# Copies of batch 0 moved to VectorE, three ties in the order of the work, and a priority for two instructions of the feed forward

## The chip, the cores and the metric

The kernel runs on one core of a Trainium2 chip. The metric is the device time of one execution in microseconds (us); less is better. A core has TensorE (matrix products, its weight loads are listed apart), VectorE, ScalarE, GpSimd and SyncE, each with an instruction queue that it works through in order, and 16 DMA engines. The times of the kernel before are from three runs; one further execution was profiled.

## The reference

The program is pooled attention followed by a mixing step by Fourier transforms and a feed forward. Shapes: 8 batches, 8 heads, 576 rows, head size 64; 512 channels, 2048 hidden units. The two feed-forward weights come as 64-bit floats, all else as 32-bit floats.

```python
# attention: keys and values are averaged over groups of 8 rows (72 groups)
k_p = k.reshape(B, H, 72, 8, D).mean(axis=3)
v_p = v.reshape(B, H, 72, 8, D).mean(axis=3)
scores = matmul(q, k_p.transpose(0, 1, 3, 2)) / sqrt(D)
x = softmax(scores) @ v_p                    # then heads side by side: (8, 576, 512)
# mixing and feed forward
u = x + real(fft(fft(x, axis=1), axis=2))
un = (u - mean(u)) / sqrt(var(u) + 1e-6)     # over the 512 channels
out = u + maximum(un @ w_ch1, 0) @ w_ch2
```

## The kernel before

Everything is kept with channels on the partitions and rows along the free axis. Each batch b has a *front end*, the generator `fe(b)`: it loads queries and keys for four pairs of heads (g = 3, 2, 0, 1), averages the keys, makes scores (`psS`), a softmax (`t`), transposes of it (`psT`, `psV`, `psR`), the product with the averaged values (`psX`, function `values`), the Fourier transform as products with cosine and sine matrices (`psA`, `psB`, then `psQ`, `psP`), the mean and the variance. Its result is `un`, split into a high part `unh` and a low part `unl`.

The *feed forward* `ffn` runs over blocks of 288 or 384 rows and, in each, over 128 hidden units at a time (a step, f). A step makes `g` with 12 products of 128x128 weights (high with high, high with low, low with high), then `hh` = relu(g) rounded on ScalarE (L779) and `hl` = relu(g) - hh on VectorE (L780), and adds 12 products of `hh` and `hl` with the second weights to four accumulators `acc`. The second half of a step (`gemm2`) comes after the next step's `g`. Batch 0 goes through four blocks: first half and second half of its rows for f 0 to 7, then both for f 8 to 15.

The *weights* come in 34 pieces (`load_w`, `prep_w`), alternately of the first and the second matrix, 512 KB each. A piece in its staging slot (`wst`) is turned into a 32-bit float by two ScalarE activations (L196, L198) and two VectorE instructions (L201 picks the sign, L202 merges), rounded into its high half on ScalarE (L206: `w1h`, `w2h`), and GpSimd subtracts (L207). The low half is stored to memory (L208) and loaded again for each step (L217: `w1low`, `w2low`). Pieces share staging slots, so a load waits until the slot's piece has been merged.

*What sets the order.* The scheduler of the framework walks a simulated time line: on each engine it issues, of the instructions that are ready, the one that was traced first. The order within a queue is fixed when the program is built. `tc.issue_after(x)` ties what is traced within it behind `x` in the queue of `x`'s engine (only the order, without a wait for its end); instructions on other engines are not tied. `behind` holds the instructions that serve as anchors: `behind["R", 0]` is batch 0's last copy of `psR` on ScalarE, `behind["E", 0]` a subtraction on VectorE ahead of `psA`, `behind["X", 0]` the subtraction of the mean from the first half of batch 0's rows (VectorE), `behind["z", 0]` the last of the four `unl` subtractions of that half (VectorE). `HOLD` and `HOLDV` name, for a piece of weights, the anchor behind which its ScalarE activations and its L201 are tied. Batch 1's reductions on VectorE are tied behind `z` already (`apart`). Batch 0's second half (`unfold`) is tied behind `z` as well.

Batch 0's front end is traced first, then the first 11 pieces of weights, then batch 1's front end with the start of batch 2's, then the feed forward, in which each step also advances the front ends of later batches. `keep_busy` puts filler matmuls (`idle`) on TensorE at named places of batch 0's front end.

Of the kernel before, what the change touches and what calls it, by code (L numbers as in the profile page):

```python
# [55 lines left out]
BUSY = {"start": 8, "S3": 3, "S2": 7, "S0": 9, "S1": 4, "T3": 3, "T0": 6, "R": 4, "X": 10, "A": 3, "P": 6, "M": 8}  # L56

HOLD = {2: "R", 3: "R", 4: "R", 5: "R", 6: "B", 7: "B", 8: "B"}
HOLDV = {4: "E", 5: "E", 6: "X", 7: "X", 8: "X"}

EARLY = [4, 6]

# [24 lines left out]
def tile_kernel(ctx: ExitStack, tc: tile.TileContext, qt, kt, vm, vr, w1, w2, cad, cbd, mkd, out):  # L87
# [93 lines left out]
    def prep_w(n):  # L181
        if n >= len(pieces):
            return
        i, f, c, w, _ = pieces[n]
        cl = slice(c * P, (c + w) * P)
        if wide:
            st = staged.pop(n)
            hi = st[:, :, :, 1]
            halves = st.bitcast(U16)
            d0 = wk.tile([P, DM], I32, tag="w", bufs=7, name="wd")[:, 0:w * P]  # L190
            di = d0.rearrange("p (c m) -> p c m", m=P)
            dh = d0.bitcast(U16).rearrange("p (c m h) -> p c m h", m=P, h=2)
            d0 = d0.bitcast(F32)

            with tc.issue_after(behind[HOLD[n], 0].ins) if n in HOLD else ExitStack():
                nc.scalar.activation(hi.bitcast(F32), hi.bitcast(F32), AF.Copy, scale=REBIAS)  # L196

                nc.scalar.activation(dh[:, :, :, 0], st.bitcast(U8)[:, :, :, 3], AF.Copy, scale=1.0 / 32.0, bias=-15.5 / 32.0)  # L198

            with tc.issue_after(behind[HOLDV[n], 0].ins) if n in HOLDV else ExitStack():  # L200
                nc.vector.tensor_scalar(out=dh[:, :, :, 1], in0=halves[:, :, :, 3], scalar1=0x8000, scalar2=None, op0=ALU.bitwise_and)  # L201
            nc.vector.scalar_tensor_tensor(out=di, in0=hi, scalar=3, in1=di, op0=ALU.logical_shift_left, op1=ALU.bitwise_or)  # L202
        else:
            d0 = staged.pop(n)
        wh = high(i, f)[:, cl]
        nc.scalar.copy(out=wh, in_=d0)  # L206
        nc.gpsimd.tensor_tensor(out=d0, in0=d0, in1=raw(wh), op=ALU.subtract)  # L207
        nc.sync.dma_start(wls[i][:, f, cl], d0)  # L208
        for m in after.get(n, ()):
            load_w(m)  # L210
# [39 lines left out]
    def fe(b):  # L250
# [85 lines left out]
        def scores(gi, i):  # L336
# [10 lines left out]
            for c0, n in ((0, 3), (3, 2)):  # L347
                ps = bank(b, f"psS{b}_{g}_{c0}")
                for c in range(n):
                    r0 = SROW[c0 + c]  # L350
                    mm = nc.tensor.matmul(ps[:, c * W2J:(c + 1) * W2J], lhsT=q[:, r0:r0 + P], rhs=kpb[g % 2], start=True, stop=True)  # L351
                if b == 0 and c0:
                    keep_busy(BUSY[f"S{g}"], mm)
                pv = ps[:, 0:n * W2J].rearrange("p (c h j) -> p c h j", h=2, j=J)
                with apart():
                    nc.vector.tensor_reduce(out=mx[:, c0:c0 + n], in_=pv, op=ALU.max, axis=AX.X, negate=(b, g) in SM)  # L356
                if (b, g) in SM:
                    nm = mx[:, c0:c0 + n]
                    nc.vector.tensor_scalar(out=nm, in0=nm, scalar1=1.0 / 64.0, scalar2=None, op0=ALU.mult)
                    for c in range(n):  # L360
                        for h in range(2):
                            x = (slice(None), c0 + c, slice(h, h + 1))
                            nc.scalar.activation(t[:, c0 + c, h], pv[:, c, h], AF.Exp, scale=1.0 / 64.0, bias=mx[x], accum_out=sm[x])
                else:
                    nc.vector.tensor_tensor(out=t[:, c0:c0 + n], in0=pv, in1=mx[:, c0:c0 + n].unsqueeze(3).broadcast_to([P, n, 2, J]), op=ALU.subtract)  # L365
# [63 lines left out]
        def values(g):  # L429
            ah, al = st["a"][g]  # L430
            wh, wl = st["w", g]
            for cl in halves:
                ps = bank(b, f"psX{b}_{g}")[:, 0:HS]
                if b in NAT:
# [5 lines left out]
                if b == 0 and g == 1 and cl.start:  # L440
                    keep_busy(BUSY["X"], last)
                if g == 3:
                    nc.scalar.copy(out=Xb[:, O0, cl], in_=ps)
                    nc.scalar.copy(out=Xb[0:1, E1, cl], in_=ps[0:1])
                elif g == 2:
                    nc.scalar.copy(out=Xb[:, O1, cl], in_=ps)
                    nc.scalar.copy(out=Xb[0:1, O0, cl], in_=ps[0:1])
                    nc.scalar.copy(out=Xb[0:1, O1, cl], in_=Xb[0:1, E1, cl])
                else:
                    e = 2 * g  # L450
                    nc.vector.tensor_tensor(out=Xb[:, e, cl], in0=ps, in1=Xb[:, e + 1, cl], op=ALU.add)
                    nc.vector.tensor_tensor(out=Xb[:, e + 1, cl], in0=ps, in1=Xb[:, e + 1, cl], op=ALU.subtract)
# [114 lines left out]
        for i, m in enumerate(shares):  # L567
            if b:
                channels(i, m, 0)
            ps, _ = channels(i, m, 1)  # L570
            if i < 2:
                parts((AB[i],), ps, 258)
            else:
# [172 lines left out]
    def ffn(ro, nb, to, f0, f1):  # L746
# [15 lines left out]
        for f in range(f0, f1):  # L762
# [13 lines left out]
                    n += 1  # L776
            hh = wk.tile([P, 384], F32R, tag="hh", bufs=2, name="hh")[:, 0:nb]
            hl = wk.tile([P, 384], F32R, tag="hl", bufs=2, name="hl")[:, 0:nb]
            nc.scalar.activation(hh, ps, AF.Relu)  # L779
            nc.vector.scalar_tensor_tensor(out=hl, in0=ps, scalar=0.0, in1=raw(hh), op0=ALU.max, op1=ALU.subtract)  # L780
            yield
            if prev:
                gemm2(f - 1, *prev)
# [214 lines left out]
```

## Time and profile before

| | us |
|---|---|
| median of three runs | 1086.92 (1086.22 to 1087.01) |
| profiled execution | 1087.56 |
| its span, first to last instruction | 1085.6 |
| TensorE busy | 1051.1 (97%) |
| VectorE busy | 615.3 (57%) |
| ScalarE busy | 414.0 (38%) |
| GpSimd busy | 256.0 (24%) |

In the profile PE is TensorE, PEld its weight loads, DVE VectorE, ACT ScalarE, POOL GpSimd and SP SyncE. Busy time is the time that instructions cover; the idle time before an instruction is put down to what released it last. The granted clock is the share of TensorE's full clock. Matmuls overlap, so the mean time of one is longer than the distance from one to the next. L446 is line 446 of the kernel before; tiles go by their names in the program.

### The profile page before, as it was taken

The numbers are of one execution on the slowest core, as the hardware profiler recorded it, in microseconds if no ns is written. First come the engines' busy times: TensorE is split into PE (matmuls) and PEld (weight loads), VectorE is DVE, ScalarE is ACT, GpSimd is POOL, SyncE is SP. The second block draws the span as 40 slices with busy tenths as digits, with TensorE's granted clock in tenths as the row PEclk, the third lists the DMA queues.
The fourth block names the chain that finished last, engine by engine and source line by source line (L and its number), as shares of the span: only waits on it lengthen the run. The fifth ranks groups of instructions, "written<-read, shape, count | busy, mean of one in ns | idle before, by whom it ended". The sixth has DMA issues, their size and how long they took to land.

```text
span 1085.6 us, 17737 instructions
## 1 busy us (share of the span) xinstructions
PE 1051.1 (97%) x6626; PEld 1016.3 (94%) x6626; DVE 615.3 (57%) x1233; ACT 414.0 (38%) x1083; POOL 256.0 (24%) x264
## 2 busy tenths in 40 slices
PE   8878898999999999999999999999999999999998
PEld 7667688999999999999999999999999999999997
DVE  6698877855376455656376455756467434522122
ACT  5868754443244331533243431443324422311110
POOL 6626365211240032311141032300231101300000
PEclk9889999999999999999999999999999999999999
DMA  8859876655345444444444444445435333346563
GB/s 310 257 186 319 282 259 211 201 177 159 113 120 165 131 153 138 128 141 157 136 124 148 133 150 137 139 131 160 140 106 156 97 106 120 116 129 191 163 190 100
DMA packets 91909, 175.80 MB, mean 162 GB/s; under 512 B 10160, under 2 KB 17328, under 8 KB 91568
## 3 DMA queue, kind: packets, MB, share of 16 engines
q1 hardware_dynamic: 91248, 171.71, 51.0%
q0 software_dynamic: 288, 2.66, 0.6%
q8 instruction: 52, 0.85, 0.3%
q10 hardware_dynamic: 288, 0.30, 0.1%
q14 instruction: 33, 0.27, 0.1%
HBM read 156.81 MB, written 17.83 MB: 161 GB/s over the span
## 4 chain that ended last, share of the span: by engine, by line
PE 86%; DVE 5%; ACT 3%; DMA 3%; POOL 1%; issue 1%; SPq 0%; DVEq 0%; POOLq 0%; ACTq 0%
PE g L775 35%; PE acc L759 35%; PE psX L439 3%; PE psS L351 3%; PE psA L558 2%; PE psP L601 2%; PE psB L584 1%; PE psQ L601 1%; PE psT L392 1%; DMA w2l<-wd 1%; POOL wd L207 1%; DMA w1low<-w1l 1%; ACT wd L198 1%; DMA k<-in_kt 1%; PE psR L415 1%
## 5 line engine op out<-in xcount | busy, mean ns | idle before, releaser
L779 ACT ACTIVATE hh<-g 128x384 fp32r<-128x384 f32 (+1 forms) x208 | 96.6, 464 | 338.1 <-PE g L775 318.4
L780 DVE SCALAR_TENSOR_TENSOR hl<-g,hh 128x384 fp32r<-128x384 f32 (+1 forms) x208 | 108.8, 523 | 189.1 <-ACT hh L779 184.2
L759 PE MATMUL acc<-hh,w2h 128*128 128x384 f32 (+1 forms) x832 | 187.2, 327 | 0.9 <-ACT hh L779 0.7
L759 PE MATMUL acc<-hh,w2low 128*128 128x384 f32 (+1 forms) x832 | 187.3, 327 | 0.0
L775 PE MATMUL g<-unh,w1low 128*128 128x384 f32 (+1 forms) x832 | 181.1, 331 | 4.6 <-DMA w1low<-w1l 4.6
L759 PE MATMUL acc<-hl,w2h 128*128 128x384 f32 (+1 forms) x832 | 182.2, 327 | 0.9 <-DVE hl L780 0.8
L775 PE MATMUL g<-unl,w1h 128*128 128x384 f32 (+1 forms) x832 | 178.2, 328 | 3.0 <-DVE unl L646 3.0
L775 PE MATMUL g<-unh,w1h 128*128 128x384 f32 (+1 forms) x832 | 172.4, 326 | 3.1 <-DVE hl L780 2.3
L775 PEld LDWEIGHTS g<-unh,w1low 128*128 128x128 f32 x832 | 140.1, 190 | 7.8 <-DMA w1low<-w1l 5.9
L759 PEld LDWEIGHTS acc<-hh,w2h 128*128 128x128 f32 x832 | 142.9, 188 | 2.7 <-ACT hh L779 1.8
L775 PEld LDWEIGHTS g<-unh,w1h 128*128 128x128 f32 x832 | 139.7, 189 | 4.6 <-DVE hl L780 2.8
L775 PEld LDWEIGHTS g<-unl,w1h 128*128 128x128 f32 x832 | 139.9, 189 | 4.3 <-DVE unl L646 3.7
L759 PEld LDWEIGHTS acc<-hh,w2low 128*128 128x128 f32 x832 | 143.1, 188 | 0.4 <-issue 0.4
L759 PEld LDWEIGHTS acc<-hl,w2h 128*128 128x128 f32 x832 | 141.6, 189 | 2.0 <-DVE hl L780 1.8
L371 POOL TENSOR_TENSOR t<-t,sm 128x720 f32<-128x720 f32 x32 | 47.4, 1482 | 267.4 <-DVE sm L370 247.2
L286 POOL TENSOR_TENSOR k<-k 128x288 f32<-128x288 f32 (+1 forms) x56 | 37.5, 670 | 84.7 <-DMA k<-in_kt 66.5
L638 POOL TENSOR_TENSOR U<-X,U 128x576 f32<-128x576 f32 (+1 forms) x14 | 19.2, 1375 | 120.3 <-DVE X L620 119.6
L356 DVE TENSOR_REDUCE mx<-psS 128x6 f32<-128x432 f32 x64 | 33.0, 526 | 22.9 <-PE psS L351 22.5
L351 PE MATMUL psS<-kpb,q 128*128 128x144 f32 x280 | 43.3, 291 | 1.6 <-DVE t L365 1.6
L351 PEld LDWEIGHTS psS<-kpb,q 128*128 128x128 f32 x280 | 40.1, 194 | 2.2 <-DVE t L365 1.8
L368 DVE TENSOR_REDUCE sm<-t 128x10 f32<-128x720 f32 x31 | 27.9, 901 | 13.1 <-ACT t L367 12.7
L798 POOL TENSOR_TENSOR U<-U,X 128x288 f32<-128x288 f32 x2 | 1.6, 798 | 140.9 <-DVE X L793 140.9
(218 smaller groups left out, 1466.4 us busy)
## 6 DMA issues: line engine op xcount, KB each, us to landing
w1low<-w1l SPq DMA_DIRECT2D x208, 256.0 KB, 2.7
w2low<-w2l SPq DMA_DIRECT2D x208, 256.0 KB, 2.9
wst<-in_w SPq DMA_DIRECT2D x30, 512.0 KB, 5.1
k<-in_kt SPq DMA_DIRECT2D x28, 288.0 KB, 3.1
q<-in_qt SPq DMA_DIRECT2D x28, 288.0 KB, 3.4
v<-in_vm SPq DMA_DIRECT2D x28, 256.0 KB, 2.9
out<-U SPq DMA_DIRECT2D x18, 384.0 KB, 3.5
w1l<-wd SPq DMA_DIRECT2D x16, 256.0 KB, 4.6
```

What stands on the lines that cost most here:

```text
L286: behind["k" if n == 1 and src.shape[1] == J else "v", b] = nc.gpsimd.tensor_tensor(out=out if n == 1 else src[:, :, 0:n], in0=src[:, :, 0 ...
L351: mm = nc.tensor.matmul(ps[:, c * W2J:(c + 1) * W2J], lhsT=q[:, r0:r0 + P], rhs=kpb[g % 2], start=True, stop=True)
L356: nc.vector.tensor_reduce(out=mx[:, c0:c0 + n], in_=pv, op=ALU.max, axis=AX.X, negate=(b, g) in SM)
L368: nc.vector.tensor_reduce(out=sm, in_=t, op=ALU.add, axis=AX.X)
L371: ins = nc.gpsimd.tensor_tensor(out=t, in0=t, in1=sm.unsqueeze(3).broadcast_to([P, 5, 2, J]), op=ALU.mult)
L439: last = nc.tensor.matmul(ps, lhsT=w, rhs=a, start=(i == 0), stop=(i == len(mm) - 1))
L558: last = nc.tensor.matmul(ps, lhsT=w, rhs=a, start=(n == 0), stop=(n == len(mm) - 1))
L601: last = nc.tensor.matmul(ps, lhsT=w, rhs=a, start=(i == 0), stop=(i == 6))
L759: mm = nc.tensor.matmul(acc[e], lhsT=w[:, e], rhs=h, start=(f == f0 and x == 0), stop=(f == f1 - 1 and x == 2))
L775: nc.tensor.matmul(ps, lhsT=w[:, c], rhs=x[:, ti, cl], start=(n == 0), stop=(n == 11))
L779: nc.scalar.activation(hh, ps, AF.Relu)
L780: nc.vector.scalar_tensor_tensor(out=hl, in0=ps, scalar=0.0, in1=raw(hh), op0=ALU.max, op1=ALU.subtract)
```

## The change

- In `values`, the copies of `psX` into `X` for head pairs 3 and 2 run on VectorE for batch 0 (ten copies: for each half of the rows, two for g = 3 and three for g = 2). For the other batches they stay on ScalarE.
- In `prep_w`, the rounding of pieces 0 and 1 into their high halves (L206) is tied behind `behind["R", 0]` on ScalarE.
- `HOLDV` ties the sign conversion (L201) of pieces 6, 7 and 8 behind `z` instead of `X`.
- In `scores`, batch 1's first score matmul for g = 3 is tied behind batch 0's last `psA` matmul on TensorE, which `channels` now hands out as `behind["psA", b]`.
- In `ffn`, the instructions of `hh` and `hl` are traced at high priority: of the ready instructions of ScalarE and VectorE the scheduler takes them first, as if they stood at the start of the program.

No instruction is added or taken away.

```diff
--- before.py
+++ after.py
@@ -56,7 +56,7 @@
 BUSY = {"start": 8, "S3": 3, "S2": 7, "S0": 9, "S1": 4, "T3": 3, "T0": 6, "R": 4, "X": 10, "A": 3, "P": 6, "M": 8}
 
 HOLD = {2: "R", 3: "R", 4: "R", 5: "R", 6: "B", 7: "B", 8: "B"}
-HOLDV = {4: "E", 5: "E", 6: "X", 7: "X", 8: "X"}
+HOLDV = {4: "E", 5: "E", 6: "z", 7: "z", 8: "z"}
 
 EARLY = [4, 6]
 
@@ -203,7 +203,8 @@
         else:
             d0 = staged.pop(n)
         wh = high(i, f)[:, cl]
-        nc.scalar.copy(out=wh, in_=d0)
+        with tc.issue_after(behind["R", 0].ins) if n < 2 else ExitStack():
+            nc.scalar.copy(out=wh, in_=d0)
         nc.gpsimd.tensor_tensor(out=d0, in0=d0, in1=raw(wh), op=ALU.subtract)
         nc.sync.dma_start(wls[i][:, f, cl], d0)
         for m in after.get(n, ()):
@@ -348,7 +349,9 @@
                 ps = bank(b, f"psS{b}_{g}_{c0}")
                 for c in range(n):
                     r0 = SROW[c0 + c]
-                    mm = nc.tensor.matmul(ps[:, c * W2J:(c + 1) * W2J], lhsT=q[:, r0:r0 + P], rhs=kpb[g % 2], start=True, stop=True)
+
+                    with tc.issue_after(behind["psA", 0].ins) if b == 1 and g == 3 and c + c0 == 0 else ExitStack():
+                        mm = nc.tensor.matmul(ps[:, c * W2J:(c + 1) * W2J], lhsT=q[:, r0:r0 + P], rhs=kpb[g % 2], start=True, stop=True)
                 if b == 0 and c0:
                     keep_busy(BUSY[f"S{g}"], mm)
                 pv = ps[:, 0:n * W2J].rearrange("p (c h j) -> p c h j", h=2, j=J)
@@ -429,6 +432,7 @@
         def values(g):
             ah, al = st["a"][g]
             wh, wl = st["w", g]
+            copy = nc.scalar.copy if b else nc.vector.tensor_copy
             for cl in halves:
                 ps = bank(b, f"psX{b}_{g}")[:, 0:HS]
                 if b in NAT:
@@ -440,12 +444,12 @@
                 if b == 0 and g == 1 and cl.start:
                     keep_busy(BUSY["X"], last)
                 if g == 3:
-                    nc.scalar.copy(out=Xb[:, O0, cl], in_=ps)
-                    nc.scalar.copy(out=Xb[0:1, E1, cl], in_=ps[0:1])
+                    copy(out=Xb[:, O0, cl], in_=ps)
+                    copy(out=Xb[0:1, E1, cl], in_=ps[0:1])
                 elif g == 2:
-                    nc.scalar.copy(out=Xb[:, O1, cl], in_=ps)
-                    nc.scalar.copy(out=Xb[0:1, O0, cl], in_=ps[0:1])
-                    nc.scalar.copy(out=Xb[0:1, O1, cl], in_=Xb[0:1, E1, cl])
+                    copy(out=Xb[:, O1, cl], in_=ps)
+                    copy(out=Xb[0:1, O0, cl], in_=ps[0:1])
+                    copy(out=Xb[0:1, O1, cl], in_=Xb[0:1, E1, cl])
                 else:
                     e = 2 * g
                     nc.vector.tensor_tensor(out=Xb[:, e, cl], in0=ps, in1=Xb[:, e + 1, cl], op=ALU.add)
@@ -567,7 +571,7 @@
         for i, m in enumerate(shares):
             if b:
                 channels(i, m, 0)
-            ps, _ = channels(i, m, 1)
+            ps, behind["psA", b] = channels(i, m, 1)
             if i < 2:
                 parts((AB[i],), ps, 258)
             else:
@@ -776,8 +780,9 @@
                     n += 1
             hh = wk.tile([P, 384], F32R, tag="hh", bufs=2, name="hh")[:, 0:nb]
             hl = wk.tile([P, 384], F32R, tag="hl", bufs=2, name="hl")[:, 0:nb]
-            nc.scalar.activation(hh, ps, AF.Relu)
-            nc.vector.scalar_tensor_tensor(out=hl, in0=ps, scalar=0.0, in1=raw(hh), op0=ALU.max, op1=ALU.subtract)
+            with tc.high_priority():
+                nc.scalar.activation(hh, ps, AF.Relu)
+                nc.vector.scalar_tensor_tensor(out=hl, in0=ps, scalar=0.0, in1=raw(hh), op0=ALU.max, op1=ALU.subtract)
             yield
             if prev:
                 gemm2(f - 1, *prev)
```

## Rows read from the trace of the kernel before

**Rows 1.** The page: busy time, share of the span and instructions of each engine.
```profile
PE 1051.1 (97%) x6626; PEld 1016.3 (94%) x6626; DVE 615.3 (57%) x1233; ACT 414.0 (38%) x1083; POOL 256.0 (24%) x264
```

**Rows 2.** Stretches: window, length, busy us (instructions) of each engine, clock, DMA share, GB/s.
```profile
29.00:36.70 7.70, 4.69 (x27) 2.95 (x25) 1.31 (x3) 7.65 (x25) 4.64 (x9) 1.00 0.81 268
36.70:46.10 9.40, 9.36 (x37) 7.08 (x38) 8.82 (x15) 6.58 (x16) 6.87 (x8) 0.64 0.82 250
...
57.00:64.00 7.00, 4.61 (x35) 4.02 (x33) 6.90 (x17) 2.40 (x5) 0.00 (x0) 1.00 0.07 27
...
69.50:79.00 9.50, 7.79 (x34) 7.32 (x35) 9.50 (x19) 7.92 (x21) 1.97 (x2) 0.68 0.84 264
79.00:95.00 16.00, 13.26 (x89) 11.68 (x87) 15.85 (x30) 14.95 (x48) 11.28 (x7) 0.99 0.94 311
95.00:130.00 35.00, 28.29 (x183) 23.68 (x184) 27.60 (x56) 27.47 (x69) 17.44 (x15) 1.00 0.94 331
...
200.00:985.00 785.00, 785.00 (x4829) 773.56 (x4829) 438.82 (x888) 272.12 (x715) 147.31 (x137) 1.00 0.45 137
```

**Rows 3.** Who waited for whom: us in total, times, longest us.
```profile
ACT hh L779 <- PE g L775: 318.4, 144, 5.6
...
PE g L775 <- DMA w1low<-w1l: 4.6, 5, 1.5
PE psV L405 <- ACT rt L379: 3.9, 2, 2.6
PE g L775 <- DVE unl L646: 3.0, 2, 1.5
PE g L775 <- DVE hl L780: 2.3, 2, 1.9
...
PE acc L759 <- DVE hl L780: 0.8, 2, 0.5
...
PE acc L759 <- ACT hh L779: 0.7, 2, 0.5
```

**Rows 4.** Chain that ended last, 29 to 46 us: start, length, what.
```profile
29.15 0.40 ACT X L446
...
29.57 0.62 ACT w1h L206
...
33.98 0.33 ACT X L448
...
36.74 3.82 PE psX L439 x8
...
45.12 1.27 PE psS L351 x10
```

**Rows 5.** VectorE in order of time, 36 to 78 us: start, length, what, idle before.
```profile
36.00 1.01 DVE L451 TENSOR_TENSOR X<-psX,X 128x288 f32<-128x288 f32 x2 [6.29 <-PE psX L439]
...
63.35 1.13 DVE L201 TENSOR_SCALAR wd<-wst 128x512 uint16<-128x512 uint16 x3
...
67.38 1.76 DVE L202 SCALAR_TENSOR_TENSOR wd<-wst,wd 128x512 int32<-128x512 int32 x1
...
69.80 1.90 DVE L638 TENSOR_TENSOR U<-X,U 128x288 f32<-128x288 f32 x2
...
73.69 0.81 DVE L639 TENSOR_TENSOR U<-X,U 128x288 f32<-128x288 f32 x2
...
76.70 1.33 DVE L661 TENSOR_TENSOR X<-U,psM 128x1152 f32<-128x1152 f32 x1
```

**Rows 6.** Groups by line and shape: busy us, mean ns, idle before.
```profile
L451 DVE TENSOR_TENSOR X<-psX,X 128x288 f32<-128x288 f32 x28 | 12.5, 455 | 18.6 <-PE psX L439 18.2
...
L446 ACT COPY X<-psX 128x288 f32<-128x288 f32 x14 | 5.4, 386 | 9.4 <-PE psX L439 9.3
```

**Rows 7.** The same chain, 91 to 105 us.
```profile
91.52 4.91 DMA w2l<-wd
...
100.34 4.28 DMA w1low<-w1l
```

## What I expected before the result

> **What bounds the kernel now.** I read the page first: TensorE is busy 1051.1 of 1085.6 us, so 34.5 us are left in which it does nothing [rows 1]. Then the table of stretches, to see where they lie [rows 2]: from 200 to 985 us it is busy 785.00 of 785.00 at full clock, and nothing that another engine does faster can shorten that part. The loss lies ahead of 200 us: 7.70 us of time with 4.69 of work at 29 to 36.7, granted clocks of 0.64 and 0.68 in 36.7 to 46.1 and 69.5 to 79, and from 79 to 130 TensorE busy 13.26 of 16 and 28.29 of 35, while VectorE is nearly full (15.85 of 16, 27.60 of 35) and the DMA engines are at 0.94. Third, TensorE's waits by cause [rows 3]: low weight halves 4.6 us, the `rt` copy on ScalarE 3.9, `unl` 3.0, `hl` 2.3 and 0.8, `hh` 0.7. Fourth, the chain of work around batch 0's values and VectorE's list of instructions there [rows 4, 5]: from 29.15 until `psX` begins at 36.74 the chain lies on ScalarE without a gap, and VectorE meanwhile sat idle for 6.29 us. Last, the chain through the feed forward's first steps [rows 7]: it runs through the weight preparation and its round trip to memory, not through TensorE.
>
> The profiled execution took 1087.56 us, 1.96 more than its span; the median of the runs is 0.64 less. I sum against the profiled one and put the same difference on the median.
>
> **Part 1: batch 0's ten copies to VectorE, and two conversions behind `R`.** The chain on ScalarE holds six of the ten copies between 29.15 and 34.31 (first and last in [rows 4]; 0.40 + 3 x 0.29 + 0.32 + 0.33 = 1.92 us) and the two conversions `w1h` and `w2h` of pieces 0 and 1 (the first 0.62, so about 1.2). All leave the chain that ends in `wh`, on which the last eight `psX` matmuls wait: 3.1 us. The other four copies lie before it, in a stretch that waits for GpSimd anyway: nothing. The moved conversions take along their subtraction on GpSimd, the store and the reload of the low half; the first low half is wanted by step 0 near 70 us, over 30 us later, so that costs nothing. VectorE gets ten copies. How long one takes there no row shows; the nearest is the sum out of the same PSUM tile and shape, 455 ns against 386 ns for the copy on ScalarE [rows 6]; a copy has one input less, so between 386 and 455: 3.9 to 4.55 us in all. The cover is the 6.29 us of idle time ahead of the first sum [rows 5]; as that sum comes 3.1 us sooner, 3.2 are left, and 0.7 to 1.3 us of copies run over, less what slips in before 27 us. I take 0.7 of cost. The net is -2.4 us. Bounds: -1.7, and on the other side -5.0, when `rt` is copied at once, TensorE's 3.9 us of `psV` waits shrink, and the last eight `psX` matmuls (3.82 us in a stretch with clock 0.64) run at nearly full clock.
>
> The Trainium skill speaks against this part: VectorE: DVE Perf Modes, the section on the TRN2 errata, has a fixed cost plus one cycle a column for both engines, 120 cycles at 0.96 GHz on VectorE and 172 at 1.2 GHz on ScalarE out of PSUM. My estimate from it for 288 columns is 425 ns against 383; the trace agrees for ScalarE (386) and has no such copy on VectorE. By that figure each copy is dearer by 0.04 us, the ten take 4.25, and the sum would move by less than 0.2 us.
>
> **Part 2: batch 1's first score matmuls behind batch 0's last `psA`.** They stand as 1.27 us between the filler matmuls and `psA` on the chain [rows 4]. Their readers on VectorE are tied behind `z` near 69 us anyway, so nobody misses them. If they fall into TensorE's wait at 57 to 64 us, the 1.27 are won; if they land between `psA` and `psB`, nothing. I take -1.0.
>
> **Part 3: three sign conversions behind `z` instead of `X`.** Before, VectorE did three of them (1.13 us) directly after `X` and then wove their merges (the third 1.76 us) between the four `unl` subtractions [rows 5]. TensorE waited 3.0 us for `unl` in two pieces [rows 3]. The tie takes all six instructions out of that place: up to -3.0. But they are done later by the same engine, which is full from 69.5 to 95 us [rows 2], and every later `hl`, score and conversion queues behind. I take half, -1.5. Bounds: 0 (VectorE alone decides) and -6.0, when TensorE's clock no longer falls either: 0.68 over 9.5 us is 3.04 us lost.
>
> **Part 4: `hh` and `hl` first.** It matters only where TensorE waits for them: 2.3 + 0.8 + 0.7 = 3.8 us, all before 200 us [rows 3]. Later ScalarE stands waiting for `g` before most of them (144 of 208 times, 318.4 us [rows 3]), so being first changes nothing there. What is pushed back on VectorE are batch 1's scores and the weights' merges, which are due soon too; half is kept: -2.0, with bounds -3.8 and 0.
>
> **Part 5: what is given back.** Feed-forward steps that come earlier ask for low halves earlier. These come by ScalarE, VectorE, GpSimd, a store of 4.91 us and a load of 4.28 [rows 7], with the DMA engines at 0.94 from 79 to 130 us. Against it, the DMA engines stood at 0.07 from 57 to 64 us [rows 2], so the stream itself can start earlier with everything else. The 4.6 us of waits for low halves grow by 0 to 4; I take +1.0, near the lower end, because the whole front shifts together.
>
> **The sum**: -2.4 - 1.0 - 1.5 - 2.0 + 1.0 = -5.9 us. 1087.56 - 5.9 = 1081.7 profiled, 1086.92 - 5.9 = 1081.0 for the median.
>
> **The rivals.** (a) Given back in full: VectorE and the DMA engines are full from 79 to 130 us, so TensorE only comes sooner to the same weights; waits for `w1low` grow from 4.6 to about 9. For it: [rows 7] and the DMA share of 0.94. Against: the stretch begins with idle DMA engines. About -1, 1086.0. (b) Slower: behind `z` VectorE has more than the three pieces ready; if it takes the second half's unfold (1.90 + 0.81 us), its subtraction of the mean (1.33) [rows 5] and four `unl` first (like the 455 ns of [rows 6], 1.8), 5.8 us in all, pieces 6 to 8 come 5.8 us later, counted from `z`, than before. Parts 1 and 2 give 3.4 of that back. Piece 6 carries step 3, and its staging slot the load of piece 10; 2.4 us later there, with a DMA stretch at 0.94 behind it that can't catch up, and parts 3 and 4 then hidden behind that wait: +2.4, 1089.3. It decides from the point where that delay is above the gain of the start. (c) The priority changes no order that matters: -3.9, 1083.0. (d) Everything joins: both stretches of low clock go, the start gains 5.0 and `unl` with its clock 4.5, and `hl` 2.5: -12, 1075.
>
> **How the numbers follow.** Forecast, 1078 to 1084.5: 0.46. (a) 0.17, (b) 0.15, (c) 0.10, (d) 0.12. The range reaches from (d) to (b), 1074.5 to 1089.0; the outer halves of both are left out. About 0.2%, 2.2 us, is what a measurement can tell from no change here: faster 0.68 (forecast, c, d), same 0.17, slower 0.15.
>
> **What the changed profile would show.** Part 1 right: the last `psX` of batch 0 ends near 38 us instead of 40.6, the copies stand on VectorE at about 0.4 us, and the 6.29 us of idle time there are gone; wrong if `psX` then waits for VectorE. Part 2: `psA` begins without `psS` before it. Part 3: no wait for `unl` at step 0, and the merges of pieces 6 to 8 behind the fourth `unl`. Part 4: the 3.8 us of waits for `hh` and `hl` below 2. Part 5: the waits for `w1low` beside 4.6 us; above 9, (a) or (b) holds, and (b) if pieces 6 to 8 are merged later than 69 us. From 200 us on TensorE should again show no gap; if it does, the priority has put something in the wrong order and the forecast fails there. The plainest test is when TensorE's last long wait ends: 5 to 6 us earlier than the 200 us of before.

## The result: 1096.9 us, slower, and the profile after

The changed kernel takes 1096.87 us, median of 4 runs (1092.88 to 1098.38), against 1086.72 for the kernel before: a ratio of 1.0086, 95% interval 1.0061 to 1.0110. The forecast was 1081.0 with a range up to 1089.0, so both the sign and the range failed. The profiled execution took 1092.88 us, span 1091.1.

The stretches of the changed kernel, in the windows of [rows 2]: window, length, busy us (instructions) of TensorE, its weight loads, VectorE, ScalarE and GpSimd, granted clock, DMA share, GB/s.

```profile
29.00:36.70 7.70, 7.41 (x45) 5.79 (x43) 4.61 (x14) 6.66 (x17) 5.06 (x8) 1.00 0.95 353
36.70:46.10 9.40, 4.31 (x22) 4.16 (x23) 9.34 (x13) 5.24 (x13) 6.59 (x6) 0.64 0.85 271
57.00:64.00 7.00, 4.96 (x34) 4.25 (x34) 6.40 (x16) 2.27 (x6) 0.00 (x0) 1.00 0.01 2
69.50:79.00 9.50, 8.47 (x44) 8.40 (x44) 9.50 (x18) 7.09 (x16) 5.64 (x4) 0.64 0.90 307
79.00:95.00 16.00, 10.58 (x65) 10.16 (x63) 13.66 (x23) 14.77 (x46) 13.33 (x9) 0.79 1.00 348
95.00:130.00 35.00, 29.61 (x177) 24.80 (x175) 28.00 (x62) 27.48 (x69) 13.79 (x13) 0.92 0.92 321
200.00:985.00 785.00, 780.17 (x4765) 766.45 (x4764) 432.94 (x874) 266.67 (x706) 146.74 (x137) 1.00 0.44 135
```

Three things are to be seen. From 29 to 36.7 us TensorE now works 7.41 of 7.70 us, but directly behind it only 4.31 of 9.40, where it had worked 9.36. From 79 to 95 us it works 10.58 of 16 at a clock of 0.79, where it had 13.26 at 0.99, and the DMA engines are full. And from 200 to 985 us, where before has not one gap, 4.83 us are idle. TensorE's waits of the changed kernel, by cause (us in total, times, longest us):

```profile
PE g L779 <- DMA w1low<-w1l: 7.5, 3, 3.5
PE psA L562 <- ACT f L515: 5.4, 1, 5.4
PE acc L763 <- DVE hl L785: 3.5, 1, 3.5
...
PE psS L354 <- DVE X L665: 2.4, 1, 2.4
PE g L779 <- DVE unl L650: 2.2, 2, 1.3
...
PE acc L763 <- ACT hh L784: 0.6, 1, 0.6
```

Against [rows 3], `psV`'s wait for `rt` fell from 3.9 to 0.2 us, `unl` at step 0 is gone (the 2.2 us of `unl` here are another wait, at 822 to 827 us), and in their place stand 5.4 us for `f`, 3.5 in one piece for `hl`, and 7.5 for `w1low` instead of 4.6.

**Where the time came from.** A program is best followed by the feed forward's own products: 4992 matmuls (`g` and `acc`), of which I note when the nth starts. Up to product 1200 and up to product 4200 the same amount of front-end work lies behind TensorE in every kernel (but for a dummy product or two, and in e12 for 12 front-end products that come behind the first mark instead of ahead), so those two marks can be compared directly. The times are read to 0.1 us, so differences of them are good to 0.1. Before reaches product 1200 at 332.0 us and needs 641.8 us from there to 4200. The changed kernel reaches it at 328.7, 3.3 earlier, and needs 650.6. So in the profile the front gained 3.3 us, and then 8.8 were lost where nothing should have changed: 5.5 in all, and the spans differ by 5.5 (1091.1 - 1085.6). In the median of the runs the loss is 10.2. If the late loss is the same in each execution, which only the profiled one shows, the front did not gain in most of them.

The late loss lies at one place. The chain of work that ended last in the changed kernel, 814 to 832 us (start, length, what):

```profile
815.67 0.14 PE psM L661
...
815.91 1.35 DVE X L665
817.26 0.81 DVE sm L371
818.07 1.86 DVE acc L809 x4
819.94 1.25 DVE X L665
...
822.25 1.39 DVE U L810 x3
...
823.76 1.39 DVE unl L650
...
826.04 1.02 DVE unl L650
...
827.11 4.26 PE g L779 x14
```

These are batch 6's rows: `psM` gives their mean, VectorE subtracts it (L665) and makes `unl` (L650), and the feed forward's `g` reads them. Feed-forward products from number 3457 on need them, and in TensorE's queue batch 6's last `psM` stands exactly behind product 3456. At the same moment a block of the feed forward ends, and VectorE also has its eight accumulator operations (L809 and L810), a softmax and batch 7's scores to do, in between. TensorE stands still. The same work on VectorE in the kernel before (start, length, instruction):

```profile
807.17 1.34 DVE L661 TENSOR_TENSOR X<-U,psM 128x1152 f32<-128x1152 f32 x1
...
809.10 1.29 DVE L661 TENSOR_TENSOR X<-U,psM 128x1152 f32<-128x1152 f32 x1
...
811.13 1.43 DVE L646 TENSOR_TENSOR unl<-X,unh 128x576 fp32r<-128x576 f32 x2 [0.74 <-ACT unh L645]
...
823.10 1.50 DVE L804 TENSOR_TENSOR acc<-acc,rb 128x384 f32<-128x384 f32 x3 [2.92 <-PE acc L759]
```

There the last `psM` stands behind product 3388, 68 products or 11.8 us (68 x 0.174, a 384-column product's pace at full clock) ahead of the need, and the rows are ready 10 us before the accumulator operations begin. Of the changed kernel's 8.8 us, 7.8 lie between 818.0 and 831.2 us: ten `psS` and 24 `g` matmuls start in these 13.2 us, which at their pace at full clock (0.124 and 0.174 us from start to start) would be 5.4. Of the 7.8, 4.6 are idle time in three pieces. Then ten `g`, from 827.5 to 830.4 us, start 0.32 us apart instead of 0.174; the granted clock is 0.67 at 828 to 832 us. The rest is slower starts around the waits, and about 1 us is spread over the other products.

### The profile page after: what moved, and what is told of

Read it like the earlier page. It is cut to its first block, busy times and chain, and to the rows that moved or that the text cites. A ratio compares the mean times of both kernels' runs of the same rounds, so it can differ in the third digit from the quotient of the medians.

```text
span 1091.1 us, 17716 instructions
## 1 busy us (share of the span) xinstructions
PE 1051.3 (96%) x6626; PEld 1019.7 (93%) x6626; DVE 616.7 (57%) x1243; ACT 410.1 (38%) x1073; POOL 256.7 (24%) x264
## 4 chain that ended last, share of the span: by engine, by line
PE 87%; DVE 6%; DMA 4%; issue 1%; ACT 1%; POOL 0%; SPq 0%; DVEq 0%; POOLq 0%; ACTq 0%
PE acc L763 36%; PE g L779 36%; PE psX L443 3%; PE psS L354 3%; PE psA L562 2%; PE psP L605 2%; PE psB L588 1%; PE psQ L605 1%; PE psT L395 1%; DMA wst<-in_w 1%; DMA w1low<-w1l 1%; DVE wd L202 1%; PE psR L418 1%; DVE wd L201 1%; DMA w1l<-wd 1%
## 5 line engine op out<-in xcount | busy, mean ns | idle before, releaser
L763 PE MATMUL acc<-hh,w2h 128*128 128x384 f32 (+1 forms) x832 | 189.8, 330 | 0.6 <-ACT hh L784 0.6
L779 PE MATMUL g<-unh,w1low 128*128 128x384 f32 (+1 forms) x832 | 178.7, 330 | 7.6 <-DMA w1low<-w1l 7.5
L779 PE MATMUL g<-unh,w1h 128*128 128x384 f32 (+1 forms) x832 | 177.8, 329 | 0.7 <-ACT unh L649 0.7
L370 ACT ACTIVATE t<-t 128x720 f32<-128x720 f32 x31 | 24.9, 803 | 36.4 <-DVE t L368 36.3
```

Of the source, the lines that this page charges most:

```text
L370: nc.scalar.activation(t, t, AF.Exp, scale=1.0 / 64.0)
L763: mm = nc.tensor.matmul(acc[e], lhsT=w[:, e], rhs=h, start=(f == f0 and x == 0), stop=(f == f1 - 1 and x == 2))
L779: nc.tensor.matmul(ps, lhsT=w[:, c], rhs=x[:, ti, cl], start=(n == 0), stop=(n == 11))
```

## The experiments

Three theories at first. **O**: the built order of the later batches is the whole loss. **W**: the weights, pushed back by the ties behind `z`, lose it in the front. **P**: the priority of `hh` and `hl` pushes the front ends back. The table is the outcome; "psM 6" is the number of feed-forward products ahead of batch 6's last `psM` in TensorE's queue (the expectations count to the first of the four, 16 fewer: 3372 for 3388, 3440 for 3456). Behind product 1200 the matmuls stand in one and the same order on TensorE in before, e6, e7, e10 and e15, and in another that e2, e5 and e14 share; ahead of it the order differs from kernel to kernel (e15 is e10 again). The two columns of us come from the profiled execution, the medians and ratios from all runs. In the last two groups of runs (e9 to e15) the kernel before itself varied more, medians of 1087.7 and 1087.8, so the ratios are what to compare there.

| kernel | parts | psM 6 | product 1200 at | 1200 to 4200 | median | ratio to before (95%) |
|---|---|---|---|---|---|---|
| before | none | 3388 | 332.0 | 641.8 | 1086.7 | 1 |
| after | 1 2 3 4 | 3456 | 328.7 | 650.6 | 1096.9 | 1.0086 (1.0061-1.0110) |
| e2 | 1 3 4 | 3388 | 331.4 | 641.9 | 1090.1 | 1.0036 (1.0022-1.0050) |
| e3 | 4 | 3456 | 332.1 | 650.6 | 1097.0 | 1.0101 (1.0081-1.0120) |
| e4 | 1 2 4 | 3456 | 331.1 | 650.5 | 1096.0 | 1.0086 (1.0061-1.0111) |
| e5 | 1 2 3 4, a dummy more | 3388 | 332.2 | 642.0 | 1092.9 | 1.0048 (1.0032-1.0064) |
| e6 | 1 3 | 3388 | 335.9 | 641.8 | 1091.0 | 1.0038 (1.0026-1.0051) |
| e7 | 1 | 3388 | 328.3 | 641.8 | 1086.1 | 0.9998 (0.9989-1.0007) |
| e8 | 1 2 3 | 3456 | 332.3 | 649.0 | 1094.9 | 1.0080 (1.0062-1.0097) |
| e9 | 1 2, a dummy more | 3388 | 332.4 | 641.8 | 1089.6 | 1.0009 (0.9987-1.0032) |
| e10 | 1 4, a dummy more | 3388 | 329.9 | 641.8 | 1084.6 | 0.9964 (0.9942-0.9986) |
| e11 | 1 2 4, a dummy more | 3388 | 333.9 | 641.7 | 1088.5 | 1.0006 (0.9983-1.0030) |
| e12 | 1, piece 6 early | 3440 | 341.5 | 647.6 | 1099.6 | 1.0104 (1.0063-1.0145) |
| e13 | 1 4 | 3456 | 328.8 | 650.5 | 1094.1 | 1.0065 (1.0043-1.0088) |
| e14 | 1 2 3 4, a dummy less | 3388 | 336.6 | 642.0 | 1092.6 | 1.0054 (1.0032-1.0075) |
| e15 | e10 again | 3388 | 331.0 | 641.8 | 1084.4 | 0.9971 (0.9953-0.9989) |

**e1, batch 6's front end earlier by hand.** It lets batch 6's front end start two places earlier (a feed-forward step has two). It then overwrites rows that batch 4's last steps still read, so part of those steps is computed from other rows.

```diff
-free = {1: 0, 2: 64, 3: 128, 4: 160, 5: 224, 6: 256, 7: 320}
+free = {1: 0, 2: 64, 3: 128, 4: 160, 5: 224, 6: 254, 7: 320}
```

> The whole change stays; only the place from which batch 6's front end goes on is set 2 positions earlier (254 instead of 256), so TensorE's queue is the same as in the changed kernel until batch 6. There batch 6's last psM comes after 3176 feed-forward products instead of 3440, where its rows are wanted at 3456. Theory O (the later order: the front of the changed kernel is some 4.8 us ahead until 720 us, and all of the loss comes from batch 6's rows being ready too late, at 817 to 831 us): 10 us less than the changed kernel's profiled 1092.9, so about 1082, with no wait of TensorE from 200 to 985 us. Theory W (the weights in front: pieces 6 to 8 done late, low halves late): the time stays at 1090 or more. Theory P (hh and hl at the highest priority push the front ends back in all steps): 1090 or more as well.

Measured: 1108.5 us, where O expected about 1082 and no wait. The edit moved batch 6's last `psM` from behind product 3456 to behind 3190, and its front end was crammed together: TensorE waited 4.5 us for `f`, 2.0 for `R` and 1.1 for `f` again between 730 and 785 us, and the clock was 0.50 from 760 to 770. W and P expected 1090 or more, but not for this reason, so it decides nothing between the theories. It shows that a front end can also stand too early and too close.

**e2, without the tie on the scores (part 2).**

```diff
-with tc.issue_after(behind["psA", 0].ins) if b == 1 and g == 3 and c + c0 == 0 else ExitStack():
-    mm = nc.tensor.matmul(...)
+mm = nc.tensor.matmul(...)
```

> The change without part 2 (batch 1's first scores are not tied behind psA). In the built program batch 6's last psM then comes after 3372 feed-forward products, as before the change, though parts 1, 3 and 4 are all in. Theory O: 1080 to 1084, no wait for unl after 200 us. Theory W: about 1095, as pieces 6 to 8 are as late as in the changed kernel. Theory P: about 1095, as the priority is in.

Measured: 1090.1. Its built order puts batch 6 back behind 3388 products, and 1200 to 4200 takes 641.9 us as in before. The late loss is gone although the priority and the ties behind `z` are still there, where W and P expected it unchanged. But 3.4 us of loss remain in the runs, against O's 1080 to 1084: there is a second loss, and the profile leaves no place for it behind product 1200.

**e3, the priority alone on the kernel before (part 4).**

```diff
-nc.scalar.activation(hh, ps, AF.Relu)
-nc.vector.scalar_tensor_tensor(out=hl, ...)
+with tc.high_priority():
+    nc.scalar.activation(hh, ps, AF.Relu)
+    nc.vector.scalar_tensor_tensor(out=hl, ...)
```

> The kernel before with part 4 alone. In the built program batch 6's last psM comes after 3440 feed-forward products, just as in the changed kernel. Theory O: slower than before by about what the late rows cost, 5 to 10 us: 1091 to 1097, with waits for unl near 820 us. Theory W: no slower than before, 1083 to 1087. Theory P: slower, 1090 or more.

Measured: 1097.0. O and P hit, W missed: none of the ties on the weights is in it. 1200 to 4200 took 650.6 us.

**e4, without the ties behind `z` (part 3).**

```diff
-HOLDV = {4: "E", 5: "E", 6: "z", 7: "z", 8: "z"}
+HOLDV = {4: "E", 5: "E", 6: "X", 7: "X", 8: "X"}
```

> The change without part 3: the sign conversions of pieces 6 to 8 are tied behind X again. In the built program batch 6's last psM still comes after 3440 feed-forward products. Theory O: no gain, 1091 to 1098. Theory W: pieces 6 to 8 come 3 to 4 us earlier, the waits for low halves fall from 7.5 us below 5, the time to about 1085. Theory P: 1091 or more.

Measured: 1096.0, 650.5 us from 1200 to 4200. W alone fails again.

**e5, the changed kernel with one dummy product more.** The kernel keeps TensorE occupied in batch 0's waits with short products that nobody reads. One of those counts is changed, far ahead of the later batches. Nothing else is touched.

```diff
-BUSY = {... "T0": 6, ...}
+BUSY = {... "T0": 7, ...}
```

> The changed kernel with one more of TensorE's dummy products (7 in place of 6 behind batch 0's psT of group 0, one short 128x128 product about 27 us into the span); not one other line differs. In the built program TensorE's front is unchanged, but the later batches' front ends stand earlier between the feed forward's products: batch 6's last psM has 3372 products ahead of it, as in before, and not 3440. Theory O (the loss of the later batches is set by where the built order puts batch 6's rows, whatever edit tips it; it was worth 8.8 us between feed-forward products 1200 and 4200, at equal TensorE work): those 3000 products take 642 us as in before and not 650.6, and the time falls to 1086-1090. Theory P (the priority itself pushes the front ends back) and theory W (weights in the front): the priority and the weights are untouched, so 1095-1098.

Measured: 1092.9. The 3000 products from 1200 to 4200 take 642.0 us again: the 8.8 us are gone with one short product that has nothing to do with them. So the late loss belongs to the order in which the instructions were laid out: all parts of the change are in e5, and the loss is not. O's 1086 to 1090 was missed again, for up to product 1200 this kernel is slower than the changed one (332.2 against 328.7): the two orders differ for batch 1 as well, whose last `psM` stands behind 490 products here and behind 502 there.

**e6 and e7, parts 1 and 3, and part 1 alone**, both in the order of before behind product 1200. Both are the kernel before with the copies on VectorE and the conversions of pieces 0 and 1 behind `R`; e6 alone has:

```diff
-HOLDV = {4: "E", 5: "E", 6: "X", 7: "X", 8: "X"}
+HOLDV = {4: "E", 5: "E", 6: "z", 7: "z", 8: "z"}
```

> Before with parts 1 and 3 (batch 0's copies on VectorE, the two conversions behind R, pieces 6 to 8 behind z), without the tie on batch 1's scores and without the priority. Batch 6's psM has 3372 products ahead, as in before. O with the front's gain kept (the forecast's parts 1 and 3, -3.9, some of it given back): 1082-1085. P (the priority is what eats the front's gain: the kernel with parts 1, 3 and 4 and the same later order took 1090.1): 1081-1085 too. W (pieces 6 to 8 behind z make the weights late and that eats the front's gain): 1087-1091.

> Before with part 1 alone (batch 0's copies on VectorE, the two conversions behind R). Batch 6's psM has 3372 products ahead, as in before. By the forecast's part 1 -2.4 (bounds -1.7 to -5.0): 1084.3, between 1081.7 and 1085. O and P: 1082-1085. W: the ties on pieces 6 to 8 are as in before, so the gain is kept: 1082-1085, and 3 us or more below the kernel with z. If the wait for f behind the first psA eats part 1 whatever stands behind it: 1086-1088.

Measured: 1091.0 and 1086.1. Part 3 alone stands between them and costs 4.9 us by the medians, 7.6 by product 1200 in the profiles (335.9 against 328.3). W was right for the front here. VectorE's list from 61 us on, first without the tie (e7), then with it (e6): start, length, instruction.

```profile
62.04 0.67 DVE L202 SCALAR_TENSOR_TENSOR wd<-wst,wd 128x512 int32<-128x512 int32 x1
62.64 0.44 DVE L649 TENSOR_TENSOR unl<-X,unh 128x288 fp32r<-128x288 f32 x1
63.01 0.68 DVE L202 SCALAR_TENSOR_TENSOR wd<-wst,wd 128x512 int32<-128x512 int32 x1
63.61 1.52 DVE L649 TENSOR_TENSOR unl<-X,unh 128x288 fp32r<-128x288 f32 x1
65.05 1.75 DVE L202 SCALAR_TENSOR_TENSOR wd<-wst,wd 128x512 int32<-128x512 int32 x1
```

```profile
62.19 1.56 DVE L649 TENSOR_TENSOR unl<-X,unh 128x288 fp32r<-128x288 f32 x4 [0.50 <-ACT unh L648]
63.67 0.82 DVE L641 TENSOR_TENSOR U<-X,U 128x288 f32<-128x288 f32 x2
...
65.44 0.96 DVE L358 TENSOR_REDUCE mx<-psS 128x6 f32<-128x432 f32 x2
66.32 0.66 DVE L284 TENSOR_REDUCE vt<-vr 32x64 f32<-32x512 f32 x1
...
68.24 0.67 DVE L202 SCALAR_TENSOR_TENSOR wd<-wst,wd 128x512 int32<-128x512 int32 x1
...
69.18 1.27 DVE L202 SCALAR_TENSOR_TENSOR wd<-wst,wd 128x512 int32<-128x512 int32 x2
```

With the tie `unl` comes in one go, as forecast, and the first `acc` starts at 66.3 us instead of 70.3. But the merges of pieces 6 and 7 end at 68.9 and 69.9 us instead of 62.7 and 63.7, 6.2 us later, behind the second half's unfold, two score reductions and others. The bill comes in two stretches (window, length, TensorE busy, clock, DMA share, GB/s), e7 first, then e6:

```profile
79.00:95.00 16.00, 11.98 (x72) 0.89 0.96 335
...
135.00:205.00 70.00, 65.07 (x465) 1.00 0.73 229
```

```profile
79.00:95.00 16.00, 10.68 (x67) 0.79 0.99 356
...
135.00:205.00 70.00, 63.95 (x416) 0.93 0.69 218
```

At 79 to 95 us TensorE waits 5.4 us for `w1low` (2.3 in e7), and the granted clock is lower; from 135 to 205 us it waits 2.8 us for one `hl` (0.8 for two in e7), and the clock is 0.66 at 155 to 165 us. Why the second stretch follows from the first is not shown. It is not simply that every later piece is late with the sixth: VectorE merges pieces 9 and 12 even 1.2 and 0.8 us earlier than in e7, and most of the others behind the sixth 0.4 to 6.3 us later.

**e8, without the priority (parts 1 to 3).**

```diff
-with tc.high_priority():
-    nc.scalar.activation(hh, ps, AF.Relu)
-    nc.vector.scalar_tensor_tensor(out=hl, ...)
+nc.scalar.activation(hh, ps, AF.Relu)
+nc.vector.scalar_tensor_tensor(out=hl, ...)
```

> The changed kernel without part 4 (hh and hl handed over at the order's own priority); parts 1, 2 and 3 stay. The built order still has batch 6's psM behind 3440 products. O: the late 8.8 us stay, 1200 to 4200 takes about 650 us; with a front from -4 to +1: 1091-1097. P: the front ends are no longer pushed back, 1082-1086. W: no priority to move the pieces, but z stays: 1090-1097.

Measured: 1094.9, and 649.0 us from 1200 to 4200, with batch 6 behind 3456 products. P falls: the late loss is there without the priority.

**e9, e10 and e11: parts 2 and 4 on top of part 1, each and both**, with one dummy more, which in all three brings batch 6's last `psM` back behind 3388.

> Part 1 and part 2 alone (copies on VectorE, two conversions behind R, batch 1's first scores behind psA), with the one dummy product more that keeps batch 6's psM behind 3372 products as in before; base is the kernel with part 1 alone, 1086.1. By the forecast's part 2 (-1.0): 1084-1086. If the tie on the scores is what costs in the front (with parts 1, 3 and 4 beside it, it and one dummy more added 2.8): 1088-1090. Products 1200 to 4200 take 642 us in either case.

> Part 1 and part 4 alone (copies on VectorE, two conversions behind R, hh and hl at the highest priority), with the one dummy product more; batch 6's psM behind 3372 products as in before. Base 1086.1. By the forecast's part 4 (-2.0; 0 to -3.8): 1082-1086. If the priority costs in the front by itself, by what it lets pass ahead of the weights: 1088-1091. 1200 to 4200 takes 642 us in either case; 650 would say that the priority makes the late loss after all.

> The changed kernel without part 3 (pieces 6 to 8 of the weights behind X, as in before) and with the one dummy product more, so that batch 6's psM stands behind 3372 products. It stands to the changed kernel with one dummy more (1092.9) as the kernel with part 1 alone (1086.1) to that with parts 1 and 3 (1091.0). If the ties of pieces 6 to 8 behind z are the front's loss, whatever else is there: 1087-1089. If part 3 costs only without the other parts (in the other later order, leaving it out gave 0.9): 1092-1094.

Measured, as ratios, against 0.9998 for part 1 alone: 1.0009 with the tie on the scores, 0.9964 with the priority, 1.0006 with both. The priority gains 0.34%, 3.7 us. The tie costs 0.11% on part 1, within the error, and 0.42%, 4.6 us, on top of parts 1 and 4. And e11 against e5 (the same with part 3, 1.0048) prices part 3 again: 0.42%, 4.6 us. The ratios of e9, e10 and e11 have errors of 0.22 to 0.24% each. Why the tie on the scores gains nothing is seen on TensorE, e7 first, then e9 (start, length, matmul, idle time before it and what ended it):

```profile
38.97 0.76 PE L353 MATMUL psS<-kpb,q 128*128 128x144 f32 x4 [1.73 <-DVE X L455]
41.88 2.95 PE L561 MATMUL psA<-ca,f 128*128 128x258 f32 x12 [2.15 <-ACT f L514]
...
47.70 2.50 PE L587 MATMUL psB<-ca,f 128*128 128x256 f32 x18
```

```profile
43.81 2.95 PE L562 MATMUL psA<-ca,f 128*128 128x258 f32 x12 [5.68 <-ACT f L515]
...
48.89 1.25 PE L354 MATMUL psS<-kpb,q 128*128 128x144 f32 x8
49.88 0.73 PE L588 MATMUL psB<-ca,f 128*128 128x256 f32 x4
50.46 0.41 PE L354 MATMUL psS<-kpb,q 128*128 128x144 f32 x2
50.60 1.90 PE L588 MATMUL psB<-ca,f 128*128 128x256 f32 x14
```

Once part 1 has moved `psX` ahead, `psA` waits for `f`. The scores used to run inside that wait; with the tie the wait is empty (5.68 us in one piece instead of 1.73 and 2.15 with the scores between them), and the scores, 1.66 us of them, now stand between `psA` and the bulk of `psB`, on the path. Not all of the delay seen here is the tie's: in e9 batch 0's last `psX` already ends 1.6 us later than in e7 (35.7 against 34.1), ahead of anything that is tied. In two pairs that start closer together, the changed kernel against e2 and e11 against e10, the first `g` starts 1.4 and 1.6 us later with the tie, about as much as the scores take; where the rest of the 4.6 us comes from no trace shows.

**e12, piece 6 earlier: the opposite of part 3.**

```diff
-HOLDV = {4: "E", 5: "E", 6: "X", 7: "X", 8: "X"}
+HOLDV = {4: "E", 5: "E", 6: "B", 7: "X", 8: "X"}
```

> Part 1 alone, and the opposite of part 3 for one piece: VectorE's work on piece 6 stands behind batch 0's last psB copy (B) in place of behind X, where VectorE has a hole of 2.3 us at 51.4 in the kernel with part 1 alone; pieces 7 and 8 as in before. If late pieces are what makes TensorE wait for w1low at 79 to 105 us (4.9 us in the kernel with part 1 alone) and lose clock there, an earlier piece gives part of it back: 2 to 4 us less in the front, 1082-1084. Batch 6's psM stands behind 3424 products in the built order (32 ahead of those that need it; 84 in before, 16 in the changed kernel): if that brings part of the late loss, 0 to 7 us are added, to 1091 at most. If the weights aren't the cause in the front: 1086 or more without a late loss.

Measured: 1099.6, far off. Piece 6's merge did end at 54.4 us instead of 62.7, but the whole order behind it changed too: batch 1's last `psM` fell behind 552 products instead of 501, batch 2's first `psX` began at 238 us instead of 215, and product 1200 came 13.2 us later. Two things changed at once, so it does not price an earlier piece. That stays open. It shows a margin in between, though: with batch 6's last `psM` behind 3440, 16 products ahead of the need, TensorE's waits around those rows (837 to 843 us) are 0.3 us for `unl`, 0.6 for `U` and 0.2 for `hl`, where the changed kernel, with none ahead, waits 4.6 us, and before, with 68, not at all.

**e13, e14 and e15: one dummy product, three times.** e13 is e10 with the dummy count of before; e14 the changed kernel with one dummy fewer; e15 is e10 again.

> Parts 1 and 4 alone, with TensorE's dummy products as in before (6 behind that psT, not 7): batch 6's psM falls behind 3440 products, against 3372 in the kernel with parts 1 and 4 and one dummy more (1084.6). Not one other line differs between the two. If the built order of the later batches is worth what the profiles of before and of the changed kernel say (8.8 us from product 1200 to 4200): 1200 to 4200 takes 650 us and the time is 1089-1094. If the loss of the later batches needs part 2 or 3 as well: 1083-1086.

> The changed kernel with one dummy product fewer behind the same psT (5 in place of 6), which also brings batch 6's psM back behind 3372 products. If it is the order and not the dummy's own time: as with one dummy more, 1200 to 4200 in 642 us and 1091-1094. If more dummy work there was itself what helped: 1097 or more.

> Parts 1 and 4 with one dummy product more, a second time beside the other two: 1084-1086 if the first result (0.9964 of before) holds.

Measured: 1094.1, 1092.6 and 1084.4. e13 and e15 are one 128x128 product apart and 9.7 us. TensorE's waits of e13 from 205 to 1000 us (us in total, times, longest):

```profile
PE psS L353 <- DVE X L664: 2.4, 1, 2.4
PE g L778 <- DVE unl L649: 1.4, 2, 0.9
```

It is the wait of the changed kernel, at the same place, without parts 2 and 3. e15 has none there (window, length, TensorE busy, clock, DMA share, GB/s):

```profile
205.00:700.00 495.00, 495.00 (x3061) 1.00 0.47 143
700.00:985.00 285.00, 285.00 (x1731) 1.00 0.42 128
```

And a dummy less does the same as a dummy more (e14: 642.0 us from 1200 to 4200), so it is the order and not the dummy's time. Parts 1 and 4 in the order of before are the fastest kernel of all: 0.9964 and 0.9971 of before in two measurements.

## Why the prediction was wrong, step by step

**What bounds the kernel: half right, and the half that was missing decided.** That the stretch of 785.00 busy us can't be shortened held in every kernel. That it can be lengthened was left out: a full TensorE says nothing on how much margin its inputs have. For batch 6 that margin was 68 products, 11.8 us; the rearranged order took all of it. This is the step of the sum that failed first: the late part of the program stood in it at nothing, and it cost 8.8 us in the profile. The prediction named the sign to look for (a gap behind 200 us), and the gap was there, but gave it no term and no chance, and blamed the priority for it in advance. e8 has the gap without the priority, e15 has the priority without the gap.

**Part 1: the chain was right, and most of the gain was not kept.** Batch 0's last `psX` ends at 34.1 us in e7 and 34.0 in the changed kernel, not near 38 but 6.5 us sooner than 40.6: the outer bound of -5.0 was nearer than -2.4. Then `f` is late next, which no step of the sum named, and takes most of it back: in e7 `psA` starts 4.3 us earlier than before, the first `g` 2.3 (61.62 against 63.95). That is close to the -2.4 of the sum, but by another way, so by luck. `f` and the sum `tmpE` that it is made from, first in before, then in the changed kernel (start, length, instruction):

```profile
41.94 0.75 DVE L518 TENSOR_TENSOR tmpE<-X 128x574 f32<-128x574 f32 x1
42.83 0.67 ACT L511 CAST f<-tmpE 128x580 fp32r<-128x580 f32 x1
```

```profile
38.75 2.20 DVE L522 TENSOR_TENSOR tmpE<-X 128x574 f32<-128x574 f32 x1
41.06 0.67 ACT L515 CAST f<-tmpE 128x580 fp32r<-128x580 f32 x1 [0.96 <-DVE tmpE L522]
```

So `f` came only 1.8 us sooner while `psX` came 6.5 sooner; in before it had been ready 2.6 us ahead of `psA`. One reason shows: the same `tmpE` took 2.20 us instead of 0.75. GpSimd had three instructions running beside it, where before had one; whether they slow it no run here tests.

In the runs of e7 part 1 is 0.9998, -0.2 us, with an interval of -1.2 to +0.8. Beside the priority it does show: e3 and e13 both have batch 6 behind 3456 and differ by part 1 alone, and e13 is 0.36% faster, 3.9 us, with an error of about 0.3%; product 1200 comes 3.3 us earlier. A copy's price was bounded well: here are the copies of the changed kernel by line and shape (busy us, mean ns), inside the 386 to 455 ns assumed.

```profile
L450 DVE COPY X<-psX 128x288 f32<-128x288 f32 x2 | 0.9, 442 | 0.0
L447 DVE COPY X<-psX 128x288 f32<-128x288 f32 x2 | 0.9, 435 | 0.0
```

The Trainium skill's figure for it (VectorE: DVE Perf Modes, the section on the TRN2 errata), from which I had estimated 425 ns, agrees within 4%.

**Part 2: wrong in sign.** -1.0 was forecast; e9 and e11 show between nothing and +4.6 us. The prediction named the place between `psA` and `psB` as the case that gains nothing; it came, and cost. The step that failed took the matmuls off the chain without asking what is late next. With part 1 in place it is `f`, and the scores had been free inside that wait.

**Part 3: wrong in sign, and rival (b) described it.** The waits for `unl` at step 0 did go. But the three pieces came 6.2, 6.2 and 3.6 us later, where the rival had 5.8, and in the changed kernel the merges end at 69.2 to 71.1 us, behind the 69 that were named as the sign. Priced between kernels with batch 6 behind 3388: +4.3 us on part 1 (1.0038 against 0.9998; 4.9 by the medians), +4.6 on parts 1, 2 and 4 (1.0048 against 1.0006), +7.8 on parts 1 and 4 (1.0036 against 0.9964). The sum had -1.5. With batch 6 behind 3456 the price is not there: the changed kernel and e4, which differ by part 3 alone, both stand at 1.0086 (0.9 us apart by the medians), and no trace tells why. I had given that rival 0.15 with +2.4 as its price, offset by the gains of parts 1 and 2, which the runs of e7 and e9 do not show.

**Part 4: right in size on part 1, but not by the wait that it named; lost beside part 3.** -2.0 with a bound of -3.8 was forecast; on part 1 it gains 0.34 and 0.27% in two measurements, 3.7 and 2.9 us. But the sign for it, waits for `hh` and `hl` below 2 us, did not come: from 60 to 205 us TensorE waits 7.6 us for them in e10 and 4.2 in e15, against 4.4 in e7, and neither profile reaches product 1200 earlier than e7's. So the size is right and the mechanism is not shown. On parts 1 and 3 it gains nothing measurable (1.0036 against 1.0038), although TensorE waits longer for `hh` and `hl` there (9.0 us in e6, 10.2 in e2). Why stays open.

**Part 5: the term exists, three times too small.** The waits for `w1low` grew by 2.9 us where +1.0 was taken, inside the 0 to 4 assumed. The clock of 0.79 from 79 to 95 us and of 0.92 from 95 to 130, where before had 0.99 and 1.00, came with them and had no term.

**The books** in ratios to before, each step one edit: part 1 -0.02%, part 3 +0.40, part 4 -0.02, part 2 with one dummy more +0.12, and that dummy taken out again, which is the order alone, +0.38. The sum is +0.86%, 9.3 us. So by this path a bit over half of the loss is the front, nearly all of it part 3, and the rest is the order. Each step has an error of about 0.15 to 0.3%. That the front loses something is shown by e5 and e14, which have all parts without the late loss (1.0048 and 1.0054). How it divides among the parts depends on the path: by e7, e10, e11 and e5 it is part 4 -0.34, part 2 +0.42, part 3 +0.42. And taken out of the changed kernel itself, part 3 is worth nothing (e4) and part 4 0.06% (e8). So the front's share stands, and its division among the parts is not settled. The order's own price is 8.6 to 8.8 us behind product 1200 in the profiles (7.2 in e8), but 3.5 to 10 in the runs (by the ratios 4.1 and 3.5 for after against e5 and e14; 9.7 by the medians of e13 and e15), as the two orders also treat batch 1 differently ahead of it. One thing stays open: the profiled executions of the changed kernel and of e5 were 4 and 5 us faster than their medians. e14, whose profiled execution lies at its median (1092.5 and 1092.6), may show how: its front order on TensorE is that of e5 but for one product, and it has an `hl` wait of 2.0 us and a clock of 0.94 at 175 to 205 us, where e5's profile has 0.2 and 1.00. What sets that off in one execution and not in another, no trace tells.

## What to carry to other kernels

A stretch in which the bounding engine never waits has a margin that its busy time doesn't show: before moving anything ahead of it, count how far each of its inputs is ready before its need, and check in the built order that the distance is still there afterwards; with a scheduler that lays out the whole program, an edit at 30 us can move work at 800. Price an edit only between kernels whose order elsewhere is the same, and make such a pair with a neutral edit, such as one dummy product. When a wait is removed, name what is late next, and whether work that was free inside the old wait now stands on the path.

## What the runs showed of the hardware that I had not expected

TensorE's clock falls also in the middle of the program after a short wait: in the changed kernel, at full speed for hundreds of us, it fell behind the 4.6 us of waits between 817 and 827 us: 0.67 on average at 828 to 832 us, that is partly at the lower of its two levels (1.2 of 2.4 GHz), and full again at 832 to 836. So these waits cost more than their length: 7.8 us from start to start, as worked out above, for 4.6 of waiting. And a copy of one partition out of PSUM (1x288) took VectorE as long as that of all 128: 434 to 436 against 435 to 442 ns.
